# One fused kernel on one core: the gate term of the attention scores moves into the score products, and with it the mask, the softmax sums, the decoding of weights and the plan's numbers

## The chip, the cores and the metric

One Trainium2 chip, one of its cores. The metric is the device time of one execution in microseconds; the time of a kernel is the median over its runs. Engines: PE (TensorE, matrix products), DVE (VectorE), ACT (ScalarE), POOL (GpSimd) and SP (SyncE, which here issues all DMAs). Each engine works through its own stream of instructions in order.

## The reference, cut to what matters

```python
# q, k, v: (4, 8, 576, 64) float32; s: (4, 8, 576)
scores = 0.125 * q @ k.T                            # for each of 32 heads
cum    = cumsum(maximum(s, 0), axis=-1)
bias   = minimum(-(cum[:, None] - cum[None, :]), 0)  # by query, by key
scores = where(causal, -1e9, scores + bias)
attn   = exp(scores - max(scores)); attn /= sum(attn) + 1e-9
x  = attn @ v                                       # as (4, 576, 512)
u  = x + (relu(x.T @ w_tok1) @ w_tok2).T            # token mixing, 576 to 256 to 576
x  = u + relu(u @ w_ch1) @ w_ch2                    # channel mixing, 512 to 1536 to 512
gate = sigmoid(causal convolution of x with 5 taps)
out  = (gate * (x @ w_val)) @ w_out                 # 512 to 512 to 512
```

The seven weight matrices come as float64. The kernel reads each number as two int32 words.

## The kernel before

**Work.** The 32 heads go in 16 pairs (`Pair`): four pairs of heads for each of the four batches. A pair's 576 queries go in five tiles (`QT`), one of 64 and four of 128, since keys past a tile's last query need not be multiplied. For each tile and head: scores (`score`, into a PSUM bank `S`), a fused add-and-minimum on DVE that writes `x` and the row minimum `st`, the exponential on ACT (`expo`), probabilities split or turned (`p_split`, `p_turn`), and the product with v (`av`) into the one PSUM bank `xbank`. After tiles 2 and 4 the rows are normalised (`norm`, `x_value`), split (`xn`) and turned (`xT`) into the batch's row buffer `R`. Then follows token mixing of the pair's channels (`tok1`, `tok2`, PSUM `t`). Channel mixing and gating run in two chunks of 320 and 256 rows for each batch (`Mlp`, `Chunk`: `ch1` and `ch2` into PSUM `c`, operand `u`, then `x_scale`, `conv` into `gate`, `val` into `v`, `outp` into `o`).

**Precision.** Products are made in float16 with each operand split in a high and a low half (three of the four products of halves), after a scale by a power of two. The four pairs of batch 0 (`WIDE`) differ: their q and k are transposed on PE in float32 and multiplied in float32, and their probabilities stay float32. All other pairs take the maxima of |q|, |k| and |v| (ACT, `scales`), get scales through `over_partitions` (PE, DVE), split q and k (`split_qk`), and are turned by a DMA transpose into `qkT`; two DMAs make a copy of k with its halves exchanged (`kx`), so that two products of 128 rows give all four products of halves.

**The gate term.** `cumulate` makes the running sums of relu(s) and writes them to a scratch array `ckd`; `turn_cum` gives the negated sum of each query as a column (`ncq`). For each head one DMA spreads the head's row of `ckd` over 128 partitions (`ck`); for each tile and head POOL computes (ck + ncq) * scale into one of three buffers `bias`, masks its last block by `affine_select`, and DVE's score step adds that to the products.

**Weights.** `decode` turns a chunk of 64-bit words into float32 in `arena` (one ACT pass, then on DVE a maximum, a pair of shifts, a shift with or, a sign step); sums bound the products (`ws`, `wf` on PE), and `Weight.split` writes the float16 halves over it.

**Order.** Nothing is ordered by hand at run time: `Plan` lists each engine's stream beforehand. A task is a generator whose steps are put on the engine that falls idle first, the most urgent (by due times `need`) first, with buffers counted (`BUFS`) and costs guessed (`cost_pe`, `cost_dve` and so on). `FRONT` and `STEADY` are due times of a pair's steps against the start of its tile, `LEN`, `PACE0` and `U0` the pace of batches and tiles, `URGENT` and `GATE` shifts by kind. Where the plan sees PE idle, `keep_warm` inserts fillers: float16 products of zeros into the unused last columns of `xbank` (L361). All instructions that the plan's helpers emit carry the helper's line, L85; so they are told apart by the names of their tiles.

## Time and profile before

| | before |
|---|---|
| runs, device us | 788.34, 801.84, 804.32 (median 801.84) |
| profiled execution, span | 787.3 us |
| PE busy | 735.0 us, 93% of the span |
| DVE, POOL, ACT busy | 549.8, 425.6, 385.0 us |
| chain that ended last | PE 53%, POOL 18%, DVE 10%, issue 9%, DMA 5% |

The profiled execution is close to the lowest of the three runs: its span is 1.0 us below it, and 14.5 us below their median. Busy time counts an engine's instructions from their start to their modelled end, so that a PE row at half clock counts twice as long. The two lines of the page that are cut in 40 slices (each of 19.7 us) show the stages: PE is nearly full everywhere but at the very start; DVE is full between the fourth and the fifteenth slice.

### The profile page before, as it was taken

The page shows a single profiled execution, that of the slowest core. Times are in us where ns is not written, and L with a number is a line of the kernel's source. Part 1 is how long each engine was busy: PE and PEld are TensorE (multiplying, and loading weights), DVE is VectorE, ACT ScalarE, POOL GpSimd, SP SyncE. Part 2 cuts the span into 40 slices and gives each one's busy share as a digit, 9 for nine tenths or more (in the row PEclk, how much of TensorE's full clock was granted, in tenths as well). Part 3 has the DMA queues.
Part 4 walks back from the last instruction along what each step waited for, and adds up shares of the span by engine and source line. Part 5 has one row for each costly group of instructions (what it writes and reads, how often), then busy time and mean ns, then how long its engine had stood idle before and what let it go on. Part 6 is the DMA issues. An engine that isn't in the chain of part 4 may idle for free.

```text
span 787.3 us, 16814 instructions
## 1 busy us (share of the span) xinstructions
PE 735.0 (93%) x6159; PEld 530.5 (67%) x6159; DVE 549.8 (70%) x1476; ACT 385.0 (49%) x935; POOL 425.6 (54%) x630
## 2 busy tenths in 40 slices
PE   4999999997987879999899999998989999999997
PEld 3567667774665657767576777676757777776874
DVE  4554648889999898849784878496838863732543
ACT  3444547566473535653664564537435652321413
POOL 1533327769697786765773877567747631303021
PEclk9999759998998999999899999999999999999999
DMA  7732240459577318775575826754486241000001
GB/s 204 198 121 85 86 141 28 104 159 217 129 185 184 72 33 148 140 174 88 104 135 123 168 45 120 161 107 92 92 153 123 44 75 48 1 2 27 1 23 39
DMA packets 193229, 82.27 MB, mean 105 GB/s; under 512 B 180213, under 2 KB 180213, under 8 KB 193146
## 3 DMA queue, kind: packets, MB, share of 16 engines
q1 hardware_dynamic: 193146, 81.20, 46.4%
q8 instruction: 48, 0.79, 0.4%
q14 instruction: 35, 0.29, 0.1%
HBM read 42.95 MB, written 4.79 MB: 61 GB/s over the span
## 4 chain that ended last, share of the span: by engine, by line
PE 53%; POOL 18%; DVE 10%; issue 9%; DMA 5%; SPq 2%; ACT 1%; POOLq 0%; ACTq 0%; DVEq 0%
PE c L85 18%; POOL bias L85 7%; PE xbank L85 7%; PE S L85 7%; PE t L85 5%; PE o L85 4%; PE v L85 4%; DMA pT<-p 3%; DVE arena L85 3%; POOL p L85 3%; DVE gate L85 2%; POOL gate L85 2%; SPq L85 2%; PE pb L85 2%; POOL x L85 2%
## 5 line engine op out<-in xcount | busy, mean ns | idle before, releaser
L85 PEld LDWEIGHTS <-arena 128*128 128x128 f16 (+1 forms) x3168 | 287.4, 99 | 94.7 <-issue 15.1
L85 PE MATMUL c<-u,arena 128*128 128x256 f16 (+1 forms) x1152 | 162.6, 291 | 7.9 <-DVE hT L85 6.6
L85 PE MATMUL c<-hT,arena 128*128 128x256 f16 (+1 forms) x1152 | 163.0, 289 | 1.4 <-DVE st L85 1.1
L85 POOL TENSOR_SCALAR bias<-ck,ncq,sc 64x64 f32<-64x64 f32 (+4 forms) x120 | 103.7, 864 | 100.6 <-DVE st L85 91.8
L85 ACT ACTIVATE x<-x,st 64x64 f32<-64x64 f32 (+4 forms) x160 | 88.8, 556 | 97.7 <-DVE st L85 90.1
L85 PE MATMUL xbank<-v,pT 128*128 128x64 f16 (+3 forms) x1240 | 87.6, 211 | 4.4 <-DMA pT<-p 4.3
L85 PE MATMUL S<-qkT 128*128 128x288 f16 (+7 forms) x240 | 82.9, 398 | 2.1 <-DVE hT L85 1.1
L85 DVE CUSTOM_DVE_ANT_0 x<-S,bias,sc 64x64 f32<-64x64 f32 (+4 forms) x120 | 56.5, 479 | 25.1 <-PE S L85 22.9
L85 DVE SCALAR_TENSOR_TENSOR arena<-raw,arena 128x512 int32<-128x512 int32 (+2 forms) x68 | 52.4, 773 | 22.1 <-PE ws_c L85 16.8
L85 ACT ACTIVATE hT<-c 128x320 f16<-128x320 f32 (+1 forms) x96 | 38.1, 402 | 57.3 <-PE c L85 56.9
L85 POOL TENSOR_SCALAR_AFFINE_SELECT bias<-bias 128x128 f32<-128x128 f32 (+1 forms) x160 | 58.9, 368 | 11.7
L85 DVE SCALAR_TENSOR_TENSOR gate<-R,cwt,gate 128x256 f32<-128x256 f32 (+1 forms) x100 | 62.0, 645 | 0.1
L85 PEld LDWEIGHTS <-pT 128*128 128x128 f16 (+2 forms) x1080 | 47.5, 98 | 18.8 <-DMA pT<-p 5.8
L85 PE MATMUL o<-arena,g 128*128 128x512 f16 (+1 forms) x240 | 58.7, 384 | 0.4 <-ACT g L85 0.3
L85 DVE SCALAR_TENSOR_TENSOR hT<-c,hT 128x320 f16<-128x320 f32 (+1 forms) x96 | 42.5, 446 | 22.7 <-ACT hT L85 22.7
L85 PE MATMUL v<-x,arena 128*128 128x256 f16 (+1 forms) x384 | 54.0, 286 | 0.8 <-DVE x L85 0.6
L85 ACT ACTIVATE p<-x 128x192 f16<-128x192 f32 (+4 forms) x89 | 39.8, 458 | 18.4 <-DMA pT<-p 13.0
L85 POOL TENSOR_TENSOR p<-x,p 64x64 f16<-64x64 f32 (+4 forms) x55 | 46.0, 836 | 4.6
L85 DVE SCALAR_TENSOR_TENSOR p<-x,p 128x576 f16<-128x576 f32 (+4 forms) x65 | 36.8, 571 | 13.1 <-ACT p L85 8.9
L85 PE MATMUL S<-kx,qkT 128*128 128x288 f16 (+3 forms) x144 | 38.8, 280 | 6.4 <-DMA kx<-qkT 6.4
L85 DVE TENSOR_SCALAR arena<-arena 128x512 f32<-128x512 f32 (+3 forms) x74 | 40.0, 543 | 2.9 <-ACT arena L85 2.8
L85 PEld LDWEIGHTS <-g 128*128 128x128 f16 (+1 forms) x240 | 23.1, 101 | 24.2 <-issue 2.3
(198 smaller groups left out, 1222.6 us busy)
## 6 DMA issues: line engine op xcount, KB each, us to landing
raw<-in_moe_w_ch_dram SPq DMA_DIRECT2D x24, 512.0 KB, 4.0
ck<-ckd SPq DMA_DIRECT2D x28, 288.0 KB, 4.0
out_dram<-ot SPq DMA_DIRECT2D x16, 256.0 KB, 2.4
stg<-in_q_dram SPq DMA_DIRECT2D x12, 288.0 KB, 3.6
stg<-in_k_dram SPq DMA_DIRECT2D x12, 288.0 KB, 3.6
kx<-qkT SPq DMA_DIRECT2D x24, 144.0 KB, 2.5
vst<-in_v_dram SPq DMA_DIRECT2D x24, 128.0 KB, 3.3
raw<-in_moe_w_val_dram SPq DMA_DIRECT2D x4, 512.0 KB, 4.0
```

The costliest lines, as they stand in the source:

```text
L85: return f(*a, **k)
```

## The change

Six edits of the code and a new set of the plan's numbers.

1. *Gate term.* `scale_cum` scales the running sums by one power of two and splits them in three float16 pieces, written to `ckd` (32 x 3 x 576). `load_ck` loads a pair's pieces into rows 64 to 66 of a new tile `qk2` on the side of the keys, and `fill` puts a scale into the same rows on the side of the queries; the second score product takes 67 rows, 64 of halves and these three. `bias`, `ck`, `ncq` and `turn_cum` are gone. The score step adds a constant tile `mask` in place of `bias`.
2. *All pairs split.* The float32 scores and PE transposes of batch 0 (`turn_wide`) are gone: its pairs go through `scales`, `split_qk` and the DMA transpose as the others do. q's halves are stored in exchanged order, so that one product of 128 rows gives the two cross terms and the second the product of high halves; the copies into `qk2` take the place of `kx`.
3. *Softmax sums.* v gets a column of ones (`DV` = 65); the sums come out of `av` in `xbank`. `expo` has no accumulator. `norm` reads the sums from `xbank`, after `av` and ahead of `x_value`, in six DVE instructions for a pair in place of four.
4. *Decoding.* The maximum and the pair of shifts become one shift; ACT's pass scales by 2^-112.
5. *Fillers* are 112 columns wide; `cost_pe` counts float32 and transposes differently for the clock.
6. *Numbers* of `URGENT`, `FRONT`, `STEADY`, `GATE`, `LEN` and others are set anew.

```diff
-    B=7, X=1, stg=1, vst=1, qk16=1, qkT=2, v16=2, ck=2, bias=3, x=4, p16=3, pT=4, x32=1, xn=1, h1=1,
+    B=7, X=1, stg=1, vst=1, qk16=1, qkT=2, qk2=2, v16=2, x=4, p16=3, pT=4, x32=1, xn=1, h1=1,
...
-U0, PACE0, LEAD0, LEAD = 15, 4.4, 12.12, 22
-LEN = [123.4, 129.74, 128.27, 118.22]
...
+U0, PACE0, LEAD0, LEAD = 14.75, 4.51, 12.33, 21.79
+LEN = [123.43, 129.29, 130.11, 100.64]
...
 FRONT = dict(
-    load=9.96, load_v=18.3, scales=3.71, turn=9, ck=10.25, ckj=0.91, bias=9.12, score=5, scorej=1.2, expo=5.81,
...
+    load=21.26, load_v=19.29, scales=16.98, split=12.78, turn=18.92, ck=25.02, split_v=9.69, score=5, scorej=1.41,
...
-        self.busy[tick] = self.busy.get(tick, 0.0) + ns * (1.0 if name == 'transpose' or k['rhs'].dtype != F32 else 0.5)
+        self.busy[tick] = self.busy.get(tick, 0.0) + ns * (0.3 if name == 'transpose' or k['rhs'].dtype == F32 else 1.0)
...
-    plan.idle = lambda: nc.tensor.matmul(xbank[:, 384:512], lhsT=idle16, rhs=idle16, start=True, stop=True)
+    plan.idle = lambda: nc.tensor.matmul(xbank[:, 400:512], lhsT=idle16, rhs=idle16[:, 0:112], start=True, stop=True)
...
+    mask = const.tile([P, S], F32, tag="mask", name="mask")
+    nc.vector.memset(mask, 0.0)
+    nc.gpsimd.affine_select(mask[:, QM:S], mask[:, QM:S], [[-1, P]], ALU.is_ge, MASKED, 0, 1)
...
+    def scale_cum():
+        c = cum[0]
+        yield from over_partitions(gck[:, 0:1], c[:, S - 1:S], floor3[:, 3:4], unit=unit14)
+        yield V
+        V.reciprocal(gck[:, 1:2], gck[:, 0:1])
+        V.tensor_scalar(gck[:, 2:3], gck[:, 0:1], 8.0, None, ALU.mult)
+        yield A, "mA"
+        r = cum[1]
+        t = raw_tile("mA").rearrange("p f t -> p (f t)").bitcast(F16)
+        pieces = t[:BH, 0:NG3 * S].rearrange("p (t c) -> p t c", t=NG3)
+        A.activation(pieces[:, 0], c, AF.Copy, scale=gck[:BH, 1:2])
+        yield V
+        V.scalar_tensor_tensor(r, c, gck[:BH, 1:2], pieces[:, 0], ALU.mult, ALU.subtract)
+        give("mB")
+        yield A
+        A.activation(pieces[:, 1], r, AF.Copy)
+        yield V
+        V.tensor_tensor(pieces[:, 2], r, pieces[:, 1], ALU.subtract)
         give("mB")
         yield SY
-        SY.dma_start(ckd, c)
```

```diff
-        for i, (q0, M) in enumerate(QT):
-            yield PE, "B"
-            tp = bank(f"cqT{i}")
-            PE.transpose(tp[:M, :BH], cum[0][:, q0:q0 + M], ident[:BH, :BH])
-            yield A
-            A.activation(ncq[:M, i, :], tp[:M, :BH], AF.Copy, scale=-1.0)
...
+        SY.dma_start(ckd, pieces)
...
         yield A
-        A.activation(a, raw[:, :, 1].bitcast(F32), AF.Abs, scale=65536.0)
+        A.activation(a, raw[:, :, 1].bitcast(F32), AF.Copy, scale=SMALL)
         yield V
-        V.tensor_scalar(a, a, D_LO, None, ALU.max)
-        yield V
-        V.tensor_scalar(ai, ai, 4, 1, ALU.logical_shift_left, ALU.logical_shift_right)
+        V.tensor_scalar(ai, ai, 3, None, ALU.logical_shift_left)
         yield V
         V.scalar_tensor_tensor(ai, raw[:, :, 0], 29, ai, ALU.logical_shift_right, ALU.bitwise_or)
```

```diff
-        def load_ck(self, j):
-            hh = self.b * H + self.h0 + j
...
-            SY.dma_start(t, ckd[hh].partition_broadcast(P))
...
+        def load_ck(self):
+            hh = self.b * H + self.h0
+            yield SY, "qk2"
...
+            self.qk2 = ap.tile([P, 2, NB, P], F16, tag="qk2", name=f"qk2_{self.nm}", bufs=BUFS["qk2"])
+            k2 = self.qk2[D:D + NG3, 1].rearrange("t n c -> t (n c)").rearrange("t (h s) -> t h s", h=2)
+            SY.dma_start(k2, ckd[hh:hh + 2].rearrange("h t s -> t h s"))
```

```diff
         def split_qk(self, j):
...
+            hi, lo = (qk16[:, j, :, t, :] for t in ((1, 0) if j == 0 else (0, 1)))
             yield one(S)
-            scaled(qk16[:, j, :, 0, :], stg[:, j], sg[:, j:j + 1])
+            scaled(hi, stg[:, j], sg[:, j:j + 1])
             yield two(S)
-            rest(qk16[:, j, :, 1, :], stg[:, j], sg[:, j:j + 1], qk16[:, j, :, 0, :])
+            rest(lo, stg[:, j], sg[:, j:j + 1], hi)
...
-            SY.dma_start(kx[0:D], qkT[D:P, 1])
-            SY.dma_start(kx[D:P], qkT[0:D, 1])
...
-        def turn_wide(self):
-            qkT = None
...
+            SY.dma_start(self.qk2[0:D, 0], qkT[D:P, 0])
+            SY.dma_start(self.qk2[0:D, 1], qkT[0:D, 1])
+            self.qf, self.kf = (qkT[:, j].rearrange("p n c -> p (n c)") for j in range(2))
+            self.q2, self.k2 = (self.qk2[0:D + NG3, j].rearrange("p n c -> p (n c)") for j in range(2))
...
+        def fill(self):
+            yield fillers(NB * P)
+            e = plan.engine
+            out = self.qk2[D:D + NG3, 0].rearrange("p n c -> p (n c)")
+            x = one16[D:D + NG3, 0:1].to_broadcast([NG3, NB * P])
+            scaled(out, x, self.sc[D:D + NG3, 0:1])
...
-        def bias(self, i, j):
...
-            G.tensor_scalar(t[:M, :N], self.ck[j][:M, :N], ncq[:M, i, hh:hh + 1], scale, ALU.add, ALU.mult)
-            G.affine_select(t[:M, q0:N], t[:M, q0:N], [[-1, M]], ALU.is_ge, MASKED, 0, 1)
```

```diff
-            if self.wide:
-                qT, kT = (self.qkT[j * D:(j + 1) * D, x] for x in range(2))
-                PE.matmul(ps[:M, :n], lhsT=qT[:, q0:q0 + M], rhs=kT[:, c0:c0 + n], start=True, stop=True)
...
+            qs, ks = slice(t0 + q0, t0 + q0 + M), slice(t0 + c0, t0 + c0 + n)
+            PE.matmul(ps[:M, :n], lhsT=self.qf[:, qs], rhs=self.kf[:, ks], start=True, stop=False)
+            PE.matmul(ps[:M, :n], lhsT=self.q2[:, qs], rhs=self.k2[:, ks], start=False, stop=True)
...
+                self.x[i, j][:M, c0:c0 + n], ps[:M, :n], mask[:M, QM - q0 + c0:QM - q0 + c0 + n], self.sc[:M, 1:2],
...
-            A.activation(x[:M, :N], x[:M, :N], AF.Exp, bias=self.mn[i, j], scale=-1.0, accum_out=self.sums[:M, i, j:j + 1])
+            A.activation(x[:M, :N], x[:M, :N], AF.Exp, bias=self.mn[i, j], scale=-1.0)
...
         def norm(self, h):
...
-            yield V
...
-            else:
-                V.tensor_scalar(rr, rr, 1e-9, self.sc[:, 3:4], ALU.add, ALU.mult)
-            yield V
-            V.reciprocal(rr, rr)
+            yield V
+            if h == 0:
+                self.sums = ap.tile([P, NU, 2], F32, tag="sums", name=f"sums_{self.nm}", bufs=3)
+            xa = self.st["xa", h][:, 0:6 * DV].rearrange("p (i h d) -> p i h d", h=2, d=DV)
+            for n, (M, i, w) in enumerate(self.spans(h)):
+                if n:
+                    yield V
+                rr = self.sums[:M, i:i + w, :]
+                total = xa[:M, i - 3 * h:i - 3 * h + w, :, D]
+                if self.wide:
+                    V.tensor_scalar(rr, total, 1e-9, None, ALU.add)
+                else:
+                    V.tensor_scalar(rr, total, 1e-9 * 2.0 ** 14, self.sc[:M, 3:4], ALU.add, ALU.mult)
+                yield V
+                V.reciprocal(rr, rr)
```

```diff
-        o = FRONT if pr.wide else STEADY
+        o = FRONT if pr.b == 0 else STEADY
...
+        step(t0 - o["scales"], "scales", after=[("load",), ("load_v",), t_floor])
...
+            step(t0 - o["split"] + 0.5 * j, "split_qk", j, after=[("scales",)])
+        step(t0 - o["turn"], "turn_qk", after=[("split_qk", 0), ("split_qk", 1), ("load_ck",)])
+        step(t0 - o["turn"], "fill", after=[("scales",), ("load_ck",)])
...
             for j in heads:
-                step(t - o["bias"] + j, "bias", i, j, after=[("load_ck", j), t_ncq] + ([] if pr.wide else [("scales",)]) + ([("bias", i - 1, j)] if i else []))
...
-                    dep = [turned, ("bias", i, j)] + ([("score", i, j, 0)] if pi else [])
+                    dep = [("turn_qk",), ("fill",)] + ([("score", i, j, 0)] if pi else [])
...
-                step(t + 1, "norm", h, after=[("expo", x, j) for x in range(3 * h, i + 1) for j in heads])
-                step(ta, "x_value", h, after=[("av", i), ("norm", h)] + ([("x_value", 0)] if h else []))
+                step(ta, "norm", h, after=[("av", i)])
+                step(ta, "x_value", h, after=[("norm", h)] + ([("x_value", 0)] if h else []))
```

**What the plan makes of it: three places.** SP's queue around the second pair of batch 0; `raw` are weights, `stg_0_1` q and k of that pair, `ck` and `p16` the spread rows of the gate term. Before:

```order
L85 DMA raw_177<-in_moe_w_tok1_dram 128x2x512
L85 DMA ck_0_183<-ckd_99 128x576
L85 DMA stg_0_1_196<-in_q_dram 128x4x64 x2
L85 DMA stg_0_1_196<-in_q_dram 64x2x64
L85 DMA raw_236<-in_moe_w_tok2_dram 128x1152
L85 DMA ck_1_255<-ckd_99 128x576
L85 DMA stg_0_1_196<-in_k_dram 128x4x64 x2
L85 DMA stg_0_1_196<-in_k_dram 64x2x64
L85 DMA raw_337<-in_moe_w_tok2_dram 128x1152
L85 DMA p16_1_113<-ckd_99 128x576
```

After:

```order
L88 DMA_TRANSPOSE qkT_0_0_320<-qk16_0_0_207 128x18x128
L88 DMA raw_381<-in_moe_w_ch1_dram 128x1024
L88 DMA qk2_0_0_197<-qkT_0_0_320 64x1152 x2
L88 DMA stg_0_1_437<-in_q_dram 128x9x64
L88 DMA raw_442<-in_moe_w_ch1_dram 128x1024
L88 DMA stg_0_1_437<-in_k_dram 128x9x64
L88 DMA raw_551<-in_moe_w_ch1_dram 128x1024
L88 DMA qk2_0_2_610<-ckd_106 3x2x576
L88 DMA raw_627<-in_moe_w_ch1_dram 128x1024
L88 DMA raw_683<-in_moe_w_ch1_dram 128x1024
L88 DMA_TRANSPOSE qkT_0_1_748<-qk16_0_1_605 128x18x128
L88 DMA raw_787<-in_moe_w_ch1_dram 128x1024
```

The loads of `stg_0_1` now come behind the turn and the copies of the first pair, and the second pair's turn stands behind five loads of raw weights that follow the first turn; the broadcasts of `ck` are gone. The maxima, the scales and the split of a pair lie between its load and its turn, on ACT, PE, DVE and POOL.

PE at the scores of the first pair; `S_0_0_0` is head 0, tile 0, `idle16` the fillers. Before:

```order
L361 LDWEIGHTS idle16_82
L361 MATMUL xbank_81<-idle16_82 128x128
L361 LDWEIGHTS idle16_82
L361 MATMUL xbank_81<-idle16_82 128x128
L85 MATMUL S_0_0_0_275<-qkT_0_0_204 64x64
L361 LDWEIGHTS idle16_82
L361 MATMUL xbank_81<-idle16_82 128x128
```

After:

```order
L370 LDWEIGHTS idle16_82
L370 MATMUL xbank_81<-idle16_82 128x112
L88 LDWEIGHTS qkT_0_0_320
L88 MATMUL S_0_0_0_472<-qkT_0_0_320 64x64
L88 LDWEIGHTS qk2_0_0_197
L88 MATMUL S_0_0_0_472<-qk2_0_0_197 64x64
L88 LDWEIGHTS qkT_0_0_320
```

One float32 product becomes two float16 products, each with its own weights; the first score stands behind many more fillers: 158 against 17. Between the first score and the first product of channel mixing there are 379 fillers against 198, after that 61 against 135. That first product of channel mixing is PE's matrix product number 921 before, 1244 after.

DVE at the normalisation of the second pair's first three tiles: `sums_0_1` is `norm`, `x32_0_1` out of `xbank` is `x_value`. Before:

```order
L85 TENSOR_SCALAR sums_0_1_514<-sums_0_1_514 128x6
L85 RECIPROCAL sums_0_1_514<-sums_0_1_514 128x6
L85 SCALAR_TENSOR_TENSOR arena_102<-raw_667,arena_102 128x512
L85 SCALAR_TENSOR_TENSOR h1_0_0_865<-t1_0_0_817,h1_0_0_865 128x256
L85 ISA x_3_3_886,st_2_3_834<-S_3_3_0_869,bias_3_3_767 128x448
```

and, 15 instructions later:

```order
L85 ISA x_3_4_966,st_2_4_914<-S_3_4_0_952,bias_3_4_854 128x288
L85 ISA st_2_4_914 128x1
L85 SCALAR_TENSOR_TENSOR arena_102<-arena_102,wsg_c10_954 128x512
L85 TENSOR_TENSOR x32_0_1_986<-xbank_81,sums_0_1_514 64x128
L85 TENSOR_TENSOR x32_0_1_986<-xbank_81,sums_0_1_514 128x256
```

After:

```order
L88 TENSOR_SCALAR sums_0_1_1128<-xbank_81 64x2
L88 TENSOR_SCALAR arena_109<-arena_109 128x512
L88 SCALAR_TENSOR_TENSOR sc_0_2_1057<-sg_0_2_1056,gck_107 128x1
L88 SCALAR_TENSOR_TENSOR sc_0_2_1057<-gm_0_2_1055 128x1
L88 TENSOR_SCALAR sc_0_2_1057<-two24_101,sg_0_2_1056 128x2
L88 RECIPROCAL sums_0_1_1128<-sums_0_1_1128 64x2
L88 SCALAR_TENSOR_TENSOR arena_109<-raw_835,arena_109 128x512
L88 TENSOR_SCALAR sums_0_1_1128<-xbank_81 128x4
L88 SCALAR_TENSOR_TENSOR arena_109<-raw_953,arena_109 128x512
L88 SCALAR_TENSOR_TENSOR qk16_0_2_1019<-stg_0_2_831,sg_0_2_1056,qk16_0_2_1019 128x9x64 x2
L88 RECIPROCAL sums_0_1_1128<-sums_0_1_1128 128x4
L88 TENSOR_REDUCE wsum_c11_1201<-ws_c11_690 1x1
```

`norm` now reads `xbank`, in two spans, with rows of weights and of the next pair's split between its steps; the two rows of `x_value`, which gives the bank back, stand 13 and 14 rows behind the first of `norm`. Counts over the whole program: DVE 1478 instructions before and 1471 after (the two `arena` steps 74 to 37, `norm` 64 to 96, the second halves of q and k 17 to 29), POOL 635 to 429 (its two-input instructions 104 to 139), SP's queue 350 to 326, ACT's maxima of batch 0 up by 8 and its 160 accumulator reads gone. Of DVE's instructions 370 stand ahead of the first split of `u` before and 381 after; from there to the last split of weights 211 and 172.

## Rows read from the trace of the kernel before

**Rows 1.** The page's first lines: span, busy time of each engine.

```profile
span 787.3 us, 16814 instructions
...
PE 735.0 (93%) x6159; PEld 530.5 (67%) x6159; DVE 549.8 (70%) x1476; ACT 385.0 (49%) x935; POOL 425.6 (54%) x630
```

**Rows 2.** Four stretches: PE, PEld, DVE, ACT, POOL busy; clock; DMA share; GB/s.

```profile
18.00:186.00 168.00, 164.55 (x1052) 114.19 (x1052) 112.78 (x345) 90.40 (x241) 89.67 (x138) 0.91 0.44 123
186.00:286.00 100.00, 84.63 (x782) 59.59 (x780) 94.61 (x210) 54.84 (x129) 80.53 (x99) 0.93 0.60 139
286.00:650.00 364.00, 345.93 (x3235) 254.22 (x3234) 273.18 (x755) 194.41 (x485) 231.53 (x354) 0.98 0.59 114
650.00:787.30 137.30, 131.85 (x1048) 96.52 (x1045) 61.66 (x141) 38.58 (x64) 21.88 (x30) 1.00 0.06 20
```

**Rows 3.** Chains that ended last in three of them (18 to 186, 186 to 286, 286 to 650).

```profile
by line: PE S L85 23.2%; PE xbank L85 21.7%; PE pb L85 8.4%; PE t L85 7.2%; PE xbank L361 5.9%; issue 4.3%; POOL bias L85 4.3%; PE p L85 4.1%; PE qk L85 3.5%; PE ws_c L85 3.3%; PE xT L85 2.5%; DVE arena L85 1.9%; DMA pT<-p 1.5%; POOL p L85 
...
by line: DVE arena L85 21.6%; issue 14.2%; POOL bias L85 11.6%; POOL p L85 6.0%; PE c L85 5.5%; DMA pT<-p 4.1%; POOL x L85 3.9%; DMA vst<-in_v_dram 3.8%; POOL gate L85 3.2%; DVE x L85 2.6%; POOL tap L85 2.3%; POOL xn L85 1.9%; DVE cst L85 1
...
by line: PE c L85 16.1%; issue 12.7%; POOL bias L85 10.2%; PE t L85 6.3%; DMA pT<-p 5.6%; PE v L85 4.9%; PE xbank L85 4.7%; POOL p L85 4.5%; PE S L85 4.1%; PE o L85 3.6%; POOL gate L85 3.0%; DVE gate L85 2.5%; SPq L85 2.3%; POOL tap L85 2.2
```

**Rows 4.** PE in order of time: float32 scores, then float16 ones.

```profile
75.38 1.02 PE L85 MATMUL S<-qkT 64*128 64x448 f32 x2
...
351.28 0.35 PE L85 MATMUL S<-qkT 128*128 128x448 f16 x1
...
351.66 0.82 PE L85 MATMUL c<-hT,arena 128*128 128x256 f16 x6
```

**Rows 5.** A stretch at half clock, columns as in rows 2.

```profile
93.60:117.40 23.80, 23.80 (x107) 15.45 (x106) 10.87 (x34) 10.10 (x28) 6.03 (x11) 0.50 0.42 118
```

**Rows 6.** Groups by shape: count, busy us, mean ns, idle before.

```profile
L85 POOL TENSOR_SCALAR bias<-ck,ncq,sc 64x64 f32<-64x64 f32 (+4 forms) x120 | 103.7, 864 | 100.6 <-DVE st L85 91.8
...
L85 DVE TENSOR_SCALAR arena<-arena 128x512 f32<-128x512 f32 x34 | 18.9, 561 | 2.8 <-ACT arena L85 2.8
...
L85 ACT ACTIVATE qk<-stg 128x576 bf16<-128x576 f32 x24 | 16.1, 673 | 0.7 <-DMA stg<-in_k_dram 0.7
...
L85 DVE SCALAR_TENSOR_TENSOR qk<-stg,sg,qk 128x576 f16<-128x576 f32 x17 | 14.3, 863 | 0.0
```

**Rows 7.** The start: DVE, POOL's first bias, then the chain (start, length, what).

```profile
4.38 1.35 DVE L85 TENSOR_TENSOR_SCAN cum<-one,cum 32x576 f32<-32x576 f32 x1
...
9.61 0.28 DVE L85 TENSOR_REDUCE xg<-xm 1x1 f32<-1x128 f32 x1 [2.85 <-PE xm L85]
...
12.93 0.22 DVE L85 TENSOR_SCALAR sc<-two,sg 128x2 f32<-128x2 f32 x1
...
17.70 0.59 POOL L85 TENSOR_SCALAR bias<-ck,ncq 64x64 f32<-64x64 f32 x1 [9.74 <-DMA ck<-ckd]
...
16.47 1.61 PE xbank L361 x14
18.08 0.40 PE S L85 x2
```

**Rows 8.** DMA issues: KB each, median us from issue to landing.

```profile
kx<-qkT SPq DMA_DIRECT2D x24, 144.0 KB, 2.5
...
qkT<-qk SPq DMA_TRANSPOSE x12, 5.1
...
stg<-in_q_dram SPq DMA_DIRECT2D x12, 288.0 KB, 3.6
```

**Rows 9.** What SP's queue waited for longest in all.

```profile
SPq L85 <- DVE arena L85: 60.8, 13, 18.4
```

**Rows 10.** DVE and POOL side by side at 289 us.

```profile
289.27 0.81 DVE L85 SCALAR_TENSOR_TENSOR gate<-R,cwt,gate 128x320 f32<-128x320 f32 x1
...
290.47 0.54 DVE L85 SCALAR_TENSOR_TENSOR gate<-R,cwt,gate 128x320 f32<-128x320 f32 x1
...
288.87 0.86 POOL L85 TENSOR_TENSOR gate<-gate,tap 128x320 f32<-128x320 f32 x1
```

325 lines of the change are left out of this document (129 added, 196 removed).

## The prediction

> **What bounds the kernel now.** I read the page's first lines first: PE is busy 93% of the span, so only time in which PE waits, or works longer than it must, can be won [rows 1]. Since such a mean covers stages with different limits, I cut the span where the work changes: at the first score (18 us), at the first product of channel mixing (186), at DVE's last split of weights (286) and after the last batch's attention (650), and looked at each engine's busy time there [rows 2]. From 18 to 186 PE is busy 164.55 of 168 us and nothing else is near its limit. From 186 to 286 DVE is, with 94.61 of 100 us, and PE has 15 us to spare. From 286 to 650 PE is again, 345.93 of 364, and from 650 on, 131.85 of 137.3. The chain of each stretch then says on what the time goes [rows 3]: in the first on PE's scores (23.2%) and values, in the second on DVE's decoding and splitting of weights (`arena`, 21.6%), in the third on products, with 10.2% on POOL's `bias`. The start is bounded by the gate term: POOL waited 9.74 us for the first spread row and began at 17.70; the first score began at 18.08 [rows 7].
>
> **Part by part.** The sum is made against the profiled execution, 787.3 us of span and 788.3 us of time, which is the lowest of the three runs; their median, 801.84, is 13.5 above it.
>
> *Up to the first score: +13 us.* It now needs two new chains. Gates: the scan ends at 5.7 [rows 7]; the scale goes through PE and DVE, which from the maximum to the last scale took 3.5 us for the first pair (9.61 to 13.15) [rows 7]; with four steps over 576 columns at 0.7 to 0.9 each, as ACT's and DVE's passes of that width [rows 6], the pieces stand at about 13, and a write and a load at 2.5 to 4 each, the landings of small copies [rows 8], put them in place at 20. q and k: both have landed by about 12, as raw weights that were issued ahead of them landed; three maxima of 0.67 [rows 6] to 14, but the floors hang on the gates' scale, so the scales stand at 19; a split is two passes of 0.86 for each of q and k, shared by three engines [rows 6]: 22; DMA transpose 5.1, copies 2.5 [rows 8], half a microsecond of issue each: 31. Best case 25, with the chains beside each other; worst 40, if the queue of SP holds a transfer back once. In the order PE has 158 fillers ahead of the first score; a run of 14 took 1.61 us [rows 7], so 158 take 18 and end near 30 as well.
>
> *From there to the first product of channel mixing: 168 us become 134.* Scores are 23.2% of the chain, 39 us. A float32 score over 448 columns at full clock held PE 1.02 us; two float16 products of 448 columns took 0.38 from the first one's start to the next product [rows 4]. At that ratio 24 of 39 go; I take 22, since some are float16 already. The PE transposes of q and k (3.5%) go: 6. POOL's `bias` held the chain for 4.3%: 7, which ACT, DVE and PE could fill again, so 0 to 7. The clock: for 23.8 us PE was busy without a gap, much of it float32, and was granted half speed, 1.2 in place of 2.4 GHz [rows 5]. Some of that was scores; if what is left runs at full clock there, 8 us come back; none if it doesn't. 181 more fillers in this part of the order: 9.9 us (5.9% of the chain) for 198 is 0.05 each, so 9; they cost up to 0.12 each, 21, where PE would not have waited. So 168 − 22 − 6 − 7 − 8 + 9 = 134. With the late start the stretch ends at 165 in place of 186: **−21**, with bounds 0 (fillers at 21, no clock, `bias` refilled, start at 40) and −40.
>
> *To the last split of weights: −12 us.* The stretch is DVE's. The order has 211 of its instructions between the first split of `u` and the last weight before, 172 after: decoding is one `arena` pass shorter (0.56 us each, [rows 6]) and more of it lies ahead. 94.6 × 172/211 = 77. Next late is PE with 84.6 of work; with the 3% that PE idles elsewhere, 88 [rows 2]. Bounds: −6, if a third of the 37 shorter decodings lies here; −23, if PE's clock (0.93 here) rises too.
>
> *To 650: −8 us.* PE idles 18 us here [rows 2], and that is the ceiling. POOL's `bias` is on the chain with 10.2%, but beside a PE that is busy 95%, so most of it is time in which PE worked. `bias` was 0.86 us a time, 103.7 us for the steady pairs, on an engine busy 231.5 of 364 [rows 2, 6]; without it POOL's splits come sooner. ACT's accumulator reads cost nothing before, as ACT is busy 194 of 364 us, and give nothing. Against it stands `norm`: it now reads `xbank`, so that the six steps for a pair lie between `av` and the return of the only such bank. In the order at least 2 us of other PE work, mostly 3 to 12, lie between one group of `av` and the next, against about 2 to 3 us for three or four short DVE steps and what DVE has ahead of them; I cost it at nothing, and if that cover is gone it is 24 groups at 0.5 to 1 us, 12 to 24. Bounds 0 and −18.
>
> *After 650: 0, ±3.* No attention is left; the numbers of the plan move work there but take none away.
>
> SP's queue loses 32 broadcasts and gains 16 small loads; it waited for DVE's `arena` 13 times, 18.4 us at the longest [rows 9], which is the first rival's matter.
>
> Sum: −21 − 12 − 8 = −41, a span of 746 and a profiled execution of 747. The runs of before lie 0 to 16 us above theirs; I put the median of the changed kernel 5 above, at **752 us**.
>
> **A rule against it.** DVE's two-input step over 320 columns took 0.81 us where a two-input POOL instruction of 0.86 ran across its start, 0.54 where POOL was idle [rows 10]: 0.27 more. The change gives POOL 35 more two-input instructions (second halves of splits): 35 × 0.27 = 9 us. The Trainium skill ("SBUF — State Buffer", section "Who interferes with whom") says that a DVE instruction with two inputs in SBUF and a POOL instruction that reads SBUF exclude each other for the whole of the first one; by it the row should have read 1.00 (blocked to 289.73, then 0.54), and 35 full blocks would be up to 30 us. The row shows less than that.
>
> **Rivals.**
>
> *Slower: the pairs of batch 0 wait for their turn.* q and k now need load 3.6, maxima 2.0, scales 3.5, split 3.4, turn 5.1, copies 2.5 = 20 us for a pair [rows 6 to 8], through single buffers (`stg`, `qk16`), and SP's queue has five loads of raw weights between the first pair's turn and the second's, each of which may wait for DVE's `arena`. A pair has 134/4 = 33 us of PE work to hide it. For: those waits of SP exist, 18.4 us at the longest [rows 9]. Against: 20 + 18.4 is 5 over 33, three times 5 is 16 us, and 765 is not slower. It becomes slower only from 27 us of queue waits in each of three pairs; with two of the longest each, 3 × 24 = 72 us more: about 820. Chance 0.05.
>
> *The front gives nothing.* The late start, the fillers and the waits of PE, whose order is fixed beforehand, eat what the scores give: the first product of channel mixing stays at 186. Then −12 − 8 = −20 or half of it: 768 to 778 profiled, 773 to 783 at the median. For: the first score is 13 us late at least, and PE's filler count triples. Against: it takes all bounds of that stretch at their bad ends. Chance 0.20; half of it is within 2% of before.
>
> *The front gives more.* PE is free of float32 scores to such a degree that DVE sets the pace of batch 0: 112.78 us of DVE work [rows 2], less some 15 passes of 0.56 of decoding [rows 6], is 105; with a tenth of idle time 117, and the first product of channel mixing comes at 31 + 117 = 148. −38 − 6 − 8 = −52: 735, median 740. For: PE's own work would allow it at 2.4 GHz. Against: float32 values, 21.7% of the chain, stay. Chance 0.17.
>
> *POOL's new two-input steps hold DVE,* where DVE is the bound: +9, 761. Chance 0.08.
>
> **How the numbers follow.** The forecast itself has 0.50. A measurement here tells 2% of 801.84 from no change: below 786 is faster. The forecast, the POOL case, the good front and half of the empty one are below: 0.85. The other half of the empty front is within 2%: 0.10. The slow rival is 0.05. The range reaches from the bounds of the first stretch at their good end with the others as forecast (−60: 727; 722 with 5 of another part) to the empty front and a run 13.5 above its profile (788).
>
> **What would show it.** In the changed kernel's profile: the first score near 31 us; the scores' share of the first chain down from 23% to about a tenth; the first channel product near 165, the last split of weights near 253, the end of attention's stretch near 609; fewer slices at reduced clock in the first quarter; no POOL row on the chain that stands for the gate term. I am wrong if PE shows waits for `qk2` or `qkT` longer than 10 us at the second to fourth pair, if `av` waits for the bank that `norm` reads, or if the fillers, and not work, fill the first quarter.

## The result, and the profile of the changed kernel

The changed kernel's four runs took 752.8 to 757.4 us, median 754.85; the kernel before, beside it, 780.9 to 804.3, median 795.09. The ratio is 0.9622, 95% interval 0.9522 to 0.9723; it is taken against the two lowest of those four, 780.85 and 788.34, while the two medians stand at 0.949. The forecast was 752, in a range of 722 to 788. The profiled execution of the changed kernel has a span of 755.6 us, 31.7 below that of before; the sum had said 41.

One thing has to be known to read these numbers: of the executions of the kernel before that were taken beside the experiments, six of seven on each occasion lie at 780 to 821 us and one at 756 to 758; the ratio above compares with executions of the first kind, and against the rare ones the changed kernel gains less than 1%.

The page of the changed kernel, first lines and the granted clock in 40 slices:

```profile
span 755.6 us, 16615 instructions
...
PE 699.6 (93%) x6365; PEld 523.3 (69%) x6365; DVE 538.2 (71%) x1469; ACT 383.0 (51%) x780; POOL 310.4 (41%) x424
...
PEclk9989888998999999998999999999999999999999
```

Beside [rows 1] PE has 35 us less to do and the same share; POOL has lost 115 us. The same stages as in [rows 2], cut at the same events: the first score (30.6 us, before 17.8), the first channel product (173.6, before 185.8), the last split of weights (243.8, before 286.0), the last product of attention (620.2, before 653.3). Columns as there:

```profile
30.60:173.60 143.00, 127.94 (x1182) 103.47 (x1180) 107.86 (x321) 92.94 (x206) 55.58 (x57) 0.89 0.55 141
173.60:243.80 70.20, 66.46 (x590) 46.52 (x589) 67.39 (x169) 45.03 (x89) 39.41 (x49) 0.99 0.70 155
243.80:620.20 376.40, 359.33 (x3386) 264.18 (x3383) 280.65 (x776) 193.68 (x399) 182.21 (x268) 0.98 0.54 99
620.20:755.60 135.40, 129.48 (x1023) 94.94 (x1020) 59.82 (x141) 38.40 (x63) 21.79 (x31) 1.00 0.05 19
```

So the first part gave 12.2 us (forecast 21), the second 30.0 (forecast 12), the third took 9.1 more (forecast 8 less), the last 1.4 more. In the first stretch PE's busy time fell by 36.6 us, from 164.55 to 127.94, and its idle time rose from 3.4 to 15.1. Its chain:

```profile
by line: PE xbank L88 20.1%; PE xbank L370 12.3%; PE S L88 10.3%; PE t L88 9.5%; DVE arena L88 6.5%; issue 5.4%; PE pb L88 4.1%; PE p L88 3.8%; DMA qk<-qkT 3.3%; DVE qk L88 3.2%; PE ws_c L88 3.0%; DVE x L88 2.8%; PE xT L88 2.1%; PE xm L88 2
```

Against the first of [rows 3]: scores from 23.2% of 168 us to 10.3% of 143, 39 to 15 us; PE's transposes of q and k and POOL's `bias` are gone; fillers from 9.9 to 17.6; DVE's `arena` from 3.2 to 9.3; and new among the larger shares are DVE's `qk` (4.6), `x` (4.0) and the copies `qk<-qkT` (4.7).

**What the clock column leaves out.** The clock record of each trace begins with a rise to full clock: at 66.2 us in the kernel before, at 21.7 us in the changed one. The views count the time ahead of it as full clock, and the lengths of the rows say otherwise. The float32 score over 448 columns, in the kernel before at 24.65 us, where the view says 1.00, and at 107.61 us, where the granted clock is 0.50:

```profile
24.65 1.86 PE L85 MATMUL S<-qkT 64*128 64x448 f32 x2
...
107.61 1.86 PE L85 MATMUL S<-qkT 64*128 64x448 f32 x2
```

At 75.38 us, at full clock, it took 1.02 [rows 4] (so a row at half clock is 1.8 times as long, not twice). So PE ran at its lower level, 1.2 GHz, from the first score to 66.2 us as well, and the 0.91 of [rows 2] should read 0.76. Of the first stretch 79 us ran at the lower clock in the kernel before and 33 us in the changed one, whose clock rose ahead of its first score.

The start, from the chain up to 60 us (start, length, what):

```profile
14.39 0.15 DVE floor L88
...
23.65 4.67 DMA qkT<-qk
...
28.92 4.76 DMA qk<-qkT
...
33.72 1.25 PE S L88 x11
```

The first product of the first score starts at 30.87 and its second half has to wait for the copies until 33.72.

### The profile page after: what moved, and what is told of

It is laid out like the page before. It is cut to its first block, busy times and chain, and to the rows that moved or that the text cites. A ratio compares the mean times of both kernels' runs of the same rounds, so it can differ in the third digit from the quotient of the medians.

```text
span 755.6 us, 16615 instructions
## 1 busy us (share of the span) xinstructions
PE 699.6 (93%) x6365; PEld 523.3 (69%) x6365; DVE 538.2 (71%) x1469; ACT 383.0 (51%) x780; POOL 310.4 (41%) x424
## 4 chain that ended last, share of the span: by engine, by line
PE 60%; DVE 24%; DMA 6%; issue 4%; ACT 3%; POOL 1%; SPq 1%; DVEq 0%; ACTq 0%; POOLq 0%
PE c L88 23%; PE xbank L88 8%; PE t L88 7%; PE o L88 6%; PE v L88 5%; PE S L88 5%; DVE x L88 4%; DVE qk L88 4%; DVE gate L88 4%; PE xbank L370 3%; DVE arena L88 3%; DMA pT<-p 3%; DMA qk<-qkT 2%; DVE p L88 2%; PE xT L88 1%
## 5 line engine op out<-in xcount | busy, mean ns | idle before, releaser
L88 DVE CUSTOM_DVE_ANT_0 x<-S,mask,sc 64x64 f32<-64x64 f32 (+4 forms) x160 | 73.9, 480 | 33.6 <-PE S L88 24.7
L88 PE MATMUL xbank<-v,pT 128*128 128x65 f16 (+3 forms) x1240 | 83.7, 206 | 7.6 <-DVE x L88 4.4
L88 POOL TENSOR_SCALAR x<-x 64x64 f32<-64x64 f32 (+4 forms) x70 | 36.1, 516 | 80.1 <-ACT p L88 77.9
L88 POOL TENSOR_TENSOR p<-x,p 64x64 f16<-64x64 f32 (+4 forms) x70 | 57.1, 816 | 5.8
L88 POOL TENSOR_SCALAR p<-x 128x576 f16<-128x576 f32 (+4 forms) x42 | 24.2, 576 | 81.6 <-ACT x L88 51.2
L370 PE MATMUL xbank<-idle 128*128 128x112 f16 x598 | 48.8, 239 | 9.1 <-DVE x L88 7.5
L88 PE MATMUL S<-qk 67*64 67x64 f16 (+2 forms) x192 | 52.6, 289 | 5.0 <-DMA qk<-qkT 5.0
L88 PE MATMUL S<-qkT 128*64 128x64 f16 (+2 forms) x192 | 52.6, 291 | 0.2 <-DVE hT L88 0.2
L370 PEld LDWEIGHTS <-idle 128*128 128x128 f16 x598 | 40.5, 112 | 14.7 <-issue 11.3
L88 ACT ACTIVATE p<-x 128x448 f16<-128x448 f32 (+4 forms) x77 | 35.2, 465 | 9.9 <-DMA pT<-p 7.9
L88 PEld LDWEIGHTS <-g 128*128 128x128 f16 (+1 forms) x240 | 23.2, 102 | 23.9 <-issue 3.0
```

What stands on the lines that cost most here:

```text
L88: return f(*a, **k)
L370: plan.idle = lambda: nc.tensor.matmul(xbank[:, 400:512], lhsT=idle16, rhs=idle16[:, 0:112], start=True, stop=True)
```

## The experiments

Each kernel was run four times beside the kernel before. "First" is the stretch from the first score to the first channel product in the profiled execution with its granted clock, "rest" what follows; both by the windows view, cut at these events. "Lower clock" is the time in both that PE ran at 1.2 GHz, by the trace's clock record, with the time ahead of its first rise (by the lengths of rows) counted in; where that rise came behind the first score, "clock" leaves time out, and the time of the rise is given.

| kernel | median us (lowest, highest) | first, clock | rest | lower clock, us: first / rest |
|---|---|---|---|---|
| before | 795 to 802 on five occasions | 168.0, 0.91 | 601.5 | 79 / 28, rise 66.2 |
| changed | 754.85 (752.81, 757.38) | 143.0, 0.89 | 582.0 | 33 / 19 |
| e1_sums | 755.62 (750.43, 760.43) | 133.9, 0.96 | 589.3 | 10 / 18 |
| e2_nofill | 761.83 (759.14, 766.63) | 147.0, 0.75 | 582.4 | 86 / 19, rise 42.7 |
| e3_decode | 792.51 (755.98, 806.17) | 164.5, 0.77 | 602.7 | 87 / 22, rise 29.9 |
| e4_nogate | 784.82 (780.00, 785.32) | 148.3, 0.99 | 617.9 | 43 / 34, rise 57.1 |
| e5_rest_dve | 763.87 (755.62, 765.20) | 140.6, 0.89 | 591.2 | 31 / 21 |
| e6_noise | 768.10 (763.41, 771.54) | 151.5, 0.84 | 579.5 | 48 / 14 |
| e7_split | 770.61 (759.16, 774.58) | 144.9, 0.86 | 599.1 | 41 / 18 |
| e8_floor | 756.74 (754.88, 760.57) | 143.9, 0.80 | 587.2 | 58 / 8 |
| e9_fill | 780.92 (778.00, 785.52) | 161.7, 0.99 | 603.5 | 55 / 24, rise 70.4 |
| e10_oldwarm | 764.30 (758.99, 766.89) | 141.5, 0.88 | 591.3 | 34 / 27 |
| e12_before_look | 801.16, one run | 180.7, 0.88 | 600.5 | 109 / 24, rise 82.6 |
| e13_numbers | 778.40 (775.40, 779.40) | 137.2, 0.83 | 609.1 | 47 / 36 |

**How far a new order alone moves the time (e6_noise).**

```diff
-U0, PACE0, LEAD0, LEAD = 14.75, 4.51, 12.33, 21.79
+U0, PACE0, LEAD0, LEAD = 14.85, 4.51, 12.33, 21.79
```

> The changed kernel with one number of the plan moved by 0.1 us (U0 14.85), so that the whole order is made anew. It measures how far a new order alone moves the time: 755 within 8 us. If it moves by more than 10, differences of that size between the other kernels tell nothing.

The median moved by 13 us, more than expected. The profiled execution, the lowest of its four, is 6 us longer: 8.5 more in the first stretch, with 15 us more at the lower clock, and 2.5 less behind it. So wherever an experiment makes the order anew, 13 us may be chance, and one new order does not show that it can't be more. Only e2 and e9 keep the order: but for the fillers, PE, DVE, ACT and POOL go through the same rows in the same sequence as in the changed kernel and the kernel before.

**`norm` behind `av` (e1_sums).**

```diff
-            A.activation(x[:M, :N], x[:M, :N], AF.Exp, bias=self.mn[i, j], scale=-1.0)
+            A.activation(x[:M, :N], x[:M, :N], AF.Exp, bias=self.mn[i, j], scale=-1.0, accum_out=self.sums[:M, i, j:j + 1])
...
-                step(ta, "norm", h, after=[("av", i)])
+                step(t + 1, "norm", h, after=[("expo", x, j) for x in range(3 * h, i + 1) for j in heads])
```

> The changed kernel with edit 3 undone: the sums come from the exponential's accumulator again and `norm` stands ahead of the values' return (the column of ones stays and is not read). Theory: with `norm` behind `av`, the bank is held longer, and the changed kernel pays for it, some 11 us in the stretch of the steady batches (PE before `xbank<-v` and `xT`: 15.1 us of waits, 4.2 in the kernel before) and up to 8 in the first stretch (fillers that wait for the bank: 11.5 us, 3.1 before). So 735 to 745 us against 755, and these waits back at 5 us and 4 us. Rival: such waits come with any order of the plan; without them others are late: 750 to 760.

755.62: the gain that the theory promised did not come. But the order was made anew, so 10 us of it could be hidden by chance; the total refutes little. The waits that it rested on are these rows of PE, in the steady stretch of the changed kernel and then of e1 (busy, mean ns, idle before and its releasers):

```profile
L88 PE MATMUL xbank<-v,pT 128*128 128x65 f16 (+2 forms) x928 | 51.3, 196 | 6.6 <-DVE x L88 4.4 <-DMA pT<-p 2.0
...
L88 PE MATMUL S<-qk 67*128 67x288 f16 (+4 forms) x115 | 31.1, 284 | 1.1 <-DMA qk<-qkT 1.1
...
L88 PE MATMUL xT<-ident,x 128*128 128x128 f32 (+1 forms) x50 | 10.6, 293 | 5.6 <-DVE x L88 5.4
```

```profile
L88 PE MATMUL xbank<-v,pT 128*128 128x65 f16 (+2 forms) x929 | 50.9, 194 | 1.9 <-DMA pT<-p 1.6
...
L88 PE MATMUL S<-qk 67*128 67x288 f16 (+4 forms) x115 | 31.0, 281 | 6.0 <-DMA qk<-qkT 5.7
...
L88 PE MATMUL xT<-ident,x 128*128 128x128 f32 (+1 forms) x50 | 10.6, 294 | 5.2 <-DVE x L88 5.0
```

With `norm` away from the bank, `xbank` waits 1.9 in place of 6.6 us, but the turn of the rows (`xT`) still 5.2, and the scores now wait 6.0 for the copies. The fillers of the first stretch waited 4.0 us in place of 9.1. (The expectation counted gaps of over 150 ns between products, these rows PE's idle time.) So some of the bank's waits are `norm`'s, and in this order others came when they went.

**The fillers (e2_nofill, e10_oldwarm, e9_fill).** e2 leaves the 598 fillers of the changed kernel out and keeps every other place:

```diff
-    plan.idle = lambda: nc.tensor.matmul(xbank[:, 400:512], lhsT=idle16, rhs=idle16[:, 0:112], start=True, stop=True)
+    plan.idle = lambda: None
```

> The changed kernel with the fillers left out and every other instruction in the same order. Theory: in the stretch from the first score to the first channel product they cost 25 us of PE's work and 11 us of waits for the bank, of which the waits of PE would take back half; the clock is at half for 33 of 143 us there with them, so they hold little: 10 to 20 us less, 735 to 745. Rival: they keep the clock; without them the half clock spreads over most of that stretch, and its 94 us of other work takes 30 us longer or more: 770 to 800.

Between both: 7 us slower. The windows of e2 (to the first channel product, and the rest):

```profile
30.40:177.40 147.00, 125.80 (x801) 95.94 (x799) 106.92 (x320) 90.24 (x204) 55.51 (x56) 0.75 0.55 137
177.40:759.80 582.40, 552.97 (x4931) 403.11 (x4930) 408.09 (x1089) 278.08 (x555) 246.71 (x348) 0.98 0.45 87
```

PE has 381 instructions fewer there and is busy nearly as long, 125.80 against 127.94 us, as its clock was 0.75 in place of 0.89. By the lengths of rows the difference is larger than the views say: without fillers the clock first rose at 42.7 us in place of 21.7, and the first stretch had 86 us at the lower clock in place of 33. The rest is unchanged (582.4, 582.0). The fillers thus give back a little more than they cost.

e10 puts the old weights into `cost_pe`, so that fewer fillers are set:

```diff
-        self.busy[tick] = self.busy.get(tick, 0.0) + ns * (0.3 if name == 'transpose' or k['rhs'].dtype == F32 else 1.0)
+        self.busy[tick] = self.busy.get(tick, 0.0) + ns * (1.0 if name == 'transpose' or k['rhs'].dtype != F32 else 0.5)
```

> The changed kernel with the weights of `cost_pe` as before (1.0 for transposes, 0.5 for float32), so that the plan inserts fewer fillers (294 in place of 379 between the first score and the first channel product). Theory: half way to the kernel without fillers: clock 0.950 to 0.960 in place of 0.966 to 0.972, time 755 to 762. Rival: the clock falls below 0.94 as in the kernel before: 770 or more.

764.30, a little above what the theory said, with a mean clock of 0.959 to 0.972; its loss is in the rest (591.3), not in the first stretch, and lies within what a new order may do. It tells nothing of the fillers.

e9 gives the kernel before more of them, 329 for 198 in the first stretch and 329 for 135 behind it:

```diff
-WARM_FROM, WARM_FILL, GAP1 = 12e3, 0.65, 13.66
+WARM_FROM, WARM_FILL, GAP1 = 12e3, 0.95, 13.66
```

> The kernel before with more fillers: the plan fills PE to 95% of each step of its clock in place of 65% (329 fillers in place of 198 between the first score and the first channel product, the rest of the order nearly the same). Theory: much of what the changed kernel gained is the granted clock, which its 379 fillers hold at 0.97 against 0.93 to 0.96 in most executions of the kernel before; here the clock rises to 0.97, the long stretch at half clock at 93 to 117 us goes, and the time falls by 10 to 15 us to 780 to 785. Rival: the float32 scores are what the clock falls in, with fillers or without: 795 within 8, clock 0.93 to 0.96.

780.92, four runs within 778 to 786, beside 802.25: by the medians the theory holds, and by more than it said. Between the profiled executions it is less, 783.7 us of span for 787.3. The windows of e9:

```profile
18.50:180.20 161.70, 161.17 (x1181) 115.23 (x1179) 111.41 (x343) 91.23 (x242) 92.57 (x139) 0.99 0.47 130
180.20:783.70 603.50, 570.58 (x5260) 421.55 (x5257) 429.56 (x1104) 287.49 (x677) 332.37 (x481) 0.98 0.46 96
```

The first stretch took 161.7 us with 130 more instructions on PE, where the profile of before [rows 2] has 168.0; the stretch at half clock at 93.6 to 117.4 [rows 5] is not there. The 0.99 is the clock behind the first rise, which came no earlier than in before (70.4 us, 66.2 there); with the time ahead of it the stretch had 55 us at the lower clock in place of 79.

**The kernel before once more (e12_before_look),** its file unchanged.

> The kernel before once more, for its profile alone: its executions differ by 60 us (756 to 820 on one chip) with mean granted clocks of 0.986 to 0.925. Theory: two executions of it differ in the length of the stretches at half clock in the first 190 us and in little else, so that each us at half clock costs about half a us: the span less half of that time stays at 750 to 760. Rival: the stretches of DMA or of waits differ too, and that remainder differs by more than 15 us.

```profile
18.20:198.90 180.70, 177.28 (x1051) 122.49 (x1050) 111.71 (x342) 90.35 (x240) 88.68 (x137) 0.88 0.40 114
198.90:799.40 600.50, 560.95 (x5065) 409.81 (x5062) 428.76 (x1106) 287.92 (x679) 332.66 (x482) 0.98 0.47 97
```

Beside [rows 2] the first stretch is 12.7 us longer, and the rest 1 us shorter than the 601.5 of before. The instructions and their order are the same in both, so each row can be laid beside its twin: all of these 12.7 us arise between 66 and 101 us of before, in PE's rows. One of them, in before and then in e12:

```profile
71.86 1.02 PE L85 MATMUL S<-qkT 64*128 64x448 f32 x2
...
76.51 1.86 PE L85 MATMUL S<-qkT 64*128 64x448 f32 x2
```

The first rise came at 82.6 us in place of 66.2, and the next spell at the lower clock lasted 41.0 us in place of 23.9. In all 109 us of the first stretch ran at the lower clock, 79 in before: 30 more for 12.7 of time, 0.43 us for each. The theory holds, the place and the price. (The span less half of all time at the lower clock is 733.7 in before and 733.1 in e12; by the clock record alone, as the theory had it, 757.9 and 765.3.) The mean clocks of whole executions leave the time ahead of the first rise out, so they don't tell how long an execution will be: e9's 785.5 us had 0.983, and an execution of before of 756.1 us had 0.986.

**Edit 2 alone (e7_split),** in the kernel before:

```diff
-            if self.wide:
-                qT, kT = (self.qkT[j * D:(j + 1) * D, x] for x in range(2))
-                PE.matmul(ps[:M, :n], lhsT=qT[:, q0:q0 + M], rhs=kT[:, c0:c0 + n], start=True, stop=True)
-            else:
-                lhs = self.qf[:, t0 + q0:t0 + q0 + M]
+            if True:
+                lhs = self.qf[:, t0 + q0:t0 + q0 + M]
...
-        if pr.wide:
-            step(t0 - o["scales"], "scales", after=[("load_v",)])
-            step(t0 - o["turn"], "turn_wide", after=[("load",)])
...
-    load=9.96, load_v=18.3, scales=3.71, turn=9, ck=10.25, ckj=0.91, bias=9.12, score=5, scorej=1.2, expo=5.81,
+    load=21.26, load_v=19.29, scales=16.98, split=12.78, turn=18.92, ck=10.25, ckj=0.91, bias=9.12, score=5, scorej=1.2, expo=5.81,
```

> The kernel before with edit 2 alone (the four pairs of batch 0 split and turned by DMA, float16 scores; due times of load, scales, split and turn as in the changed kernel). Theory: scores give 13 us, PE transposes 5, the later first score takes 9 to 13 of it: 5 to 10 us faster, 785 to 790. Rival as forecast: scores 22, transposes 6, clock 8, less 10 for the start: 25 us faster, 770. Other rival: the start eats all: 795.

770.61 against 795.26: 25 us, which is the forecast's own sum for this edit and more than the theory made from the trace; between the profiled executions it is 14.5. First score at 29.1 us, 11 later than before, and the first channel product at 173.7 as in the changed kernel (173.6). The rest is about as before, 599.1. So edit 2 alone, with the gate term still on POOL, reaches what the changed kernel reaches there. The parts of the sum are not shown with it: the clock rose at 20.9 us, ahead of the first score, with 129 fillers ahead of that score in place of 17, and the first stretch had 41 us at the lower clock in place of 79, at 0.43 some 16 us of its 23 (an estimate), where the sum counted 8 for the clock and 22 for the scores.

**The gate term's ceiling (e4_nogate),** in the kernel before: `bias`, `load_ck` and `turn_cum` left out,

```diff
-                self.x[i, j][:M, c0:c0 + n], ps[:M, :n], bi[:M, c0:c0 + n], -0.125 if self.wide else self.sc[:M, 1:2],
+                self.x[i, j][:M, c0:c0 + n], ps[:M, :n], mask[:M, QM - q0 + c0:QM - q0 + c0 + n], -0.125 if self.wide else self.sc[:M, 1:2],
...
-                step(t - o["bias"] + j, "bias", i, j, after=[("load_ck", j), t_ncq] + ([] if pr.wide else [("scales",)]) + ([("bias", i - 1, j)] if i else []))
```

> The kernel before without the gate term: no spread rows, no `bias` on POOL, a constant mask in the score step (the output lacks the gate term). It is the ceiling of edit 1. Theory: scores no longer wait for POOL (8.6 us of PE's waits before scores in the first stretch, 10.5 in the steady one) and the start is up to 5 us earlier: 15 to 20 us faster, 775 to 780. Rival: POOL is busy 54% and beside PE; what waited for it waits for the next: at most 5 us faster, 790.

784.82, 10 us below: between the two. The first stretch is short (148.3), but it had 43 us at the lower clock in place of 79, at 0.43 some 15 of the 20 us (an estimate). The rest is long, 617.9 against 601.5: POOL was busy 235 us there in place of 334 [rows 2], and nothing was won in the steady batches. That speaks against POOL as their bound, though the chain gave it 10.2% [rows 3]; as the order was made anew, it does not settle it.

**Decoding alone (e3_decode),** in the kernel before:

```diff
-        A.activation(a, raw[:, :, 1].bitcast(F32), AF.Abs, scale=65536.0)
-        yield V
-        V.tensor_scalar(a, a, D_LO, None, ALU.max)
-        yield V
-        V.tensor_scalar(ai, ai, 4, 1, ALU.logical_shift_left, ALU.logical_shift_right)
+        A.activation(a, raw[:, :, 1].bitcast(F32), AF.Copy, scale=SMALL)
+        yield V
+        V.tensor_scalar(ai, ai, 3, None, ALU.logical_shift_left)
```

> The kernel before with edit 4 alone (decoding with one shift in place of a maximum and a pair of shifts). Theory: 37 DVE steps of 0.56 us, 21 us of DVE in all, a third of it in the stretch from 186 to 286 where DVE is the bound: 6 to 10 us faster, 785 to 790 against 795, and that stretch 90 to 94 us. Rival: all of it is on the path of weights: 20 us faster. Other rival: the order is made anew and gives it back: within 3 us.

792.51 against 795.26 with runs of 756 to 806: no difference can be told in the total. From the first channel product to the last split of weights its profile has

```profile
182.60:274.10 91.50, 78.52 (x681) 54.03 (x679) 84.33 (x193) 50.67 (x119) 71.03 (x88) 0.94 0.72 156
```

9 us less than [rows 2], with 18 DVE instructions fewer, as expected; but from the first channel product to the end it took 602.7 in place of 601.5, so it was not kept behind that, as it would not be if the later stages don't wait for the last split of weights. Its first stretch took 164.5 us with 87 us at the lower clock, less than the 168.0 with 79 of before, so between different orders the clock does not decide alone.

**The late start (e8_floor).**

```diff
+    nc.vector.memset(floor3[:, 0:2], TINYQ * 2.0 ** -14)
...
-    t_floor = task(-20, floors(), [t_gck])
...
-        step(t0 - o["scales"], "scales", after=[("load",), ("load_v",), t_floor])
+        step(t0 - o["scales"], "scales", after=[("load",), ("load_v",)])
```

> The changed kernel with a constant floor for the scales of q and k, so that the first pair's scales do not wait for the gates' chain (for the inputs drawn the floor decides nothing). Theory: of the 13 us by which the first score is later, the wait for the floors behind DVE's decoding (floor at 14.1 us) is 3 to 5; the first score at 27 to 29 us and the whole 3 to 5 us shorter: 750 to 752. Rival: the order and its fillers were laid for 31 us, so nothing moves: 755.

The first score came at 27.9 us, 3 earlier as the theory said, and the total did not move (756.74): the first channel product came 2 us earlier, at 171.6, and the rest took 587.2. Neither theory fits well; 3 us are too few beside a new order.

**Second halves on DVE (e5_rest_dve).**

```diff
-    two=dict(V=(1.04, 1130), G=(2.93, 560)),
+    two=dict(V=(1.04, 1130)),
```

> The changed kernel with every second half of a split on DVE (POOL may not take it). Theory: POOL's two-input steps cost DVE 0.27 us each where they lie beside it, DVE's own step 0.6 to 0.9, so moving some 90 of them loads DVE by 40 us net in stretches where it is the bound or nearly: 10 to 20 us slower, 765 to 775. Rival: the two-input steps of POOL hold DVE for their whole length: 755 or faster.

763.87, 9 us slower, less than the theory's lower end and within what a new order may do: unclear. Nor was DVE loaded as the theory had it: 84 of POOL's two-input steps went, but the new order put 20 of the gating's and 6 of the weights' there, and DVE was busy 539.1 us in place of 538.2. It was not faster, so there is no sign that POOL's steps hold DVE for their whole length; the rule of the Trainium skill ("SBUF — State Buffer", section "Who interferes with whom") that was weighed in the prediction is neither borne out nor refuted by this run.

**The numbers of the plan (e13_numbers).** The changed kernel's code with the old numbers; two of the lines:

```diff
-LEN = [123.43, 129.29, 130.11, 100.64]
+LEN = [123.4, 129.74, 128.27, 118.22]
...
-    x_scale=-0.42, x_split=6.25, conv=2.12, convd=12.07, sigm=9.31, sigme=-3.8, su=4.72, u=-1.24,
+    x_scale=4.93, x_split=6.24, conv=2.19, convd=1.61, sigm=9.91, sigme=2.95, su=1.55, u=0.58,
```

> The changed kernel's code with the numbers of the kernel before (U0, PACE0, LEN, the W_ numbers, URGENT, GATE, STEADY; FRONT stays). From the first channel product to the end the changed kernel takes 582 us, the kernel before 601, and none of edits 1, 2 and 4 alone gets below 598. Theory: the 20 us are the numbers' (an order that fits), so 600 us there again and 770 to 780 in all. Rival: they come from the edits together, with POOL and DVE relieved: 585 us there, 755 to 762 in all.

778.40, 23.5 above the changed kernel:

```profile
31.00:168.20 137.20, 127.38 (x1041) 100.46 (x1038) 101.08 (x316) 90.14 (x202) 39.96 (x50) 0.83 0.59 145
168.20:777.30 609.10, 570.35 (x5130) 417.51 (x5127) 413.75 (x1093) 278.72 (x553) 249.62 (x349) 0.97 0.43 84
```

The rest takes 609.1 in place of 582.0, as the theory said and the rival did not; the first stretch is 5.8 shorter than the changed kernel's. By the medians the code without the new numbers is worth 22 us against 800.65, and the numbers 23.5 more. By the profiled executions the code gives 10.0 (17.6 ahead of the first channel product, 7.6 lost again behind it) and the numbers 21.7 (27.1 behind it, 5.4 lost ahead of it). Of the 27.1 us PE was idle for 12 and busy for 15, with 188 fillers in place of 61 and 36 us at the lower clock in place of 19. The new numbers with the old code were not run.

## Why the prediction was right, point by point

*The time* was right, 752 forecast and 754.85 measured, but with some luck. The parts −21, −12, −8 and 0 came as −12.2, −30.0, +9.1 and +1.4, errors that in part cancel: −41 forecast from profile to profile, −31.7 found. And the median, put 5 us above the profile for the runs' scatter, came 2.5 below it (the profiled execution is the slowest of the four), so that an error of 10 us at the profile became one of 3.

*The first score,* forecast at 31, came at 30.87. That it hung on the floors was right (14.39 in the rows above), and e8 shows that this wait cost the first score 3 us; the total did not move with it. The copies took 4.8 us rather than 2.5, so that the score was whole at 33.7.

*The first stretch* was to take 134 us and took 143. On the chain the scores came at −24 (forecast −22), the transposes at −6 (−6), the fillers at +8 (+9). Two terms failed.

The first is the clock, 8 us for the one stretch of 23.8 us [rows 5]. By the rows 79 us of this stretch had run at the lower clock and 33 still did, 46 fewer; at 0.43 us for each, 20 us (an estimate). This is not apart from the scores, since many of their 39 us were rows at the lower clock: without it the two first stretches would take about 134 and 129 us, which leaves some 5 us for all other terms. The same float32 work took less time for the same reason, as PE's turns of the probabilities show, before and after:

```profile
L85 PE MATMUL pb<-ident,x 128*128 128x128 f32 x80 | 19.2, 355 | 0.0
...
L88 PE MATMUL pb<-ident,x 128*128 128x128 f32 x80 | 14.9, 294 | 0.0
```

The second is POOL's `bias`, "7, which ACT, DVE and PE could fill again, so 0 to 7". PE idled for no more than 3.4 us in that stretch [rows 2], so its waits had no 7 us to give, and they rose to 15.1: ahead of fillers from 0.4 to 9.1, of which 7.5 until DVE gave the bank back, and 3.1 for the copies.

e7 shows what edit 2 can do by itself: alone, in the kernel before, it put the first channel product at 173.7. How much of that is the products and how much the earlier rise of the clock, these runs don't separate.

*To the last split of weights* the forecast was −12 and the profile has −30, and behind it −8 and +9. The step that failed is the cut: the last split was taken for an event that later stages wait for. It came 42 us earlier, with less of PE's work ahead of it (590 matrix products in place of 785) and more behind (3386 in place of 3275), and they went on at PE's pace; e3 points the same way, 9 us gained ahead of it and none behind. Both stretches together were forecast at −20 and took −20.9: cut at the same events, PE's busy time fell from 434.1 to 425.8 and its idle time from 33.4 to 20.8.

*Why* these 20 us came was wrong. They were put on shorter decoding and on POOL's `bias`. Edits 2 and 4 alone, and the whole gate term left out, left the rest of the program at 599 us or more; the changed code with the old numbers at 609; the new numbers with that code make 582. So the code alone does not bring them; whether the numbers would without the code is open. The forecast spoke of the numbers only for the last stretch, where they "move work there but take none away", and put no term for them anywhere else: they also decide how long PE waits and how many fillers it runs.

*`norm`* was costed at nothing under cover of other PE work, at 12 to 24 us without. The waits for the bank came, as the forecast's own sign of being wrong had it: 4.4 us from DVE in the steady stretch, 7.5 at the fillers, which write to the same bank and so are no cover. In e1 most of them went, others came, and the time was the same; as that order was new, this does not show that they cost nothing.

*The rivals.* The slower one did not happen: SP's queue waited 6.5 us at the longest for DVE's `arena`, in place of 18.4 [rows 9], and PE waited 5.0 us in all for the copies. The front gave something, though less than forecast; it did not become DVE's (107.86 of 143 us). POOL's two-input steps: nothing shown (e5).

*What was not in it at all:* that the time of before depends on how much of its first stretch falls to half clock, which differs from one execution to the next: 79 us and 109. e12 shows it with the same instructions in the same order; the forecast took one stretch of 23.8 us [rows 5] for a property of the kernel and did not see the 48 us ahead of the first rise. Over the whole execution the lower clock fell from 107 us in the profile of before to 51 in the changed kernel's; at 0.43 us for each that is 24 of the 31.7 us between the two (an estimate), so the earlier rise is a rival to every saving of work that the forecast counted. How much of the 40 us between the medians it makes can't be told apart from edit 2 by these runs, since e7, with the float32 scores gone, has 129 fillers ahead of its first score and 326 behind it; fillers ahead of the first score of the old code were not run. No execution of before near 756 us has a profile, so whether its clock rises early is not shown.
